# A written-out order for the first batch of an attention and mixer kernel, with filler matmuls, half-column loads and a thinner second batch

## The chip, the cores and the metric

The kernel runs on one core of a Trainium2 chip. A core has five engines that each work through their own instruction list in order and wait for one another by semaphores: TensorE (PE, matmuls; its weight loads are shown apart as PEld), VectorE (DVE), ScalarE (ACT), GpSimd (POOL) and SyncE (SP, which here only issues transfers). Sixteen DMA engines move data between the device memory (HBM) and the on-chip memory (SBUF). Matmuls write to PSUM, an accumulator memory of eight banks, and DVE or ACT must read ("evict") a bank before it can be used again. The metric is the time of one execution on the device in microseconds (us).

## The reference

Two stages follow each other: a cosine attention and a low-rank token mixer with a channel MLP.

```python
# attention: q, k, v are [8 batches, 12 heads, 448 positions, 64]
q_n = q / (np.linalg.norm(q, axis=-1, keepdims=True) + 1e-06)
k_n = k / (np.linalg.norm(k, axis=-1, keepdims=True) + 1e-06)
attn = softmax(np.matmul(q_n, k_n.transpose(0, 1, 3, 2)) / tau)     # tau = 0.1
x = heads_side_by_side(np.matmul(attn, v))                          # [8, 448, 768]
# mixer: U [448, 32], V [32, 448], w_ch1 [768, 3072], w_ch2 [3072, 768]
u = x + ((x.transpose(0, 2, 1) @ U) @ V).transpose(0, 2, 1)
out = u + np.maximum(u @ w_ch1, 0.0) @ w_ch2
```

Inputs and output are float32; matmul operands are bfloat16 on the chip.

## The kernel before

**Units.** The 12 heads of a batch are six *pairs* of heads; there are 48 pairs, numbered through. Pairs are loaded and normalized in *groups*: the first batch has groups of 1, 1, 2 and 2 pairs (g0 to g3), every later batch three groups of 2 (g4, g5, g6 for the second). A group's q, k and v go to staging buffers, of which there are three sets, used in turn (`gi % NST`), so group 3's q can only be loaded once group 0's q has been read.

**Work on a group** (class `Prep`, lines 206 to 269): `square` (ACT or POOL) and `reduce` (DVE) give the squared norms of the rows; `reduce(0)` also clamps them from below (line 240); `root` takes the square root as Exp(0.5 Ln(x)) on ACT; `invert` takes the reciprocal with the temperature folded in (DVE); `scale` multiplies q or k by it and rounds to bfloat16 (DVE or POOL); `values` rounds v (POOL).

**Work on a pair.** `step_T` transposes q and k: by eight PE transposes into a PSUM bank, which DVE copies to SBUF, for the first two batches, and by DMA for the later ones. `step_S` makes scores in four parts, three of two heads by 128 keys and one of the last 64 keys of both heads (c = 3), each evicted by an Exp on ACT. `step_V` multiplies by the values in two halves; its row sums come out beside them, and DVE divides (lines 352 and 353). `step_A`, `step_H` apply the low-rank mixer: A = U^T x is copied to SBUF by ACT, x transposed and A times V are summed in one bank, `up`, and this is evicted to `uE` or `uO` (even and odd batches).

**Mixing pieces.** A batch's channel MLP is 24 pieces of `steps_m1` (six matmuls of 448 columns, and a relu on ACT or DVE, whichever a running estimate finds freer) and 24 of `steps_m2` (six matmuls of 384 columns; four pieces make one output tile of one column half). A piece of the second kind needs rows of w2 of one column half only; a complete output tile needs all 24 row blocks of that half. The pieces of batch b are put into the list `fill` and handed out between the steps of the pairs of batch b + 1 by `spread`, according to the weights in `order`.

**What sets the order.** All five engines run in the order in which the Python code emits instructions. The first batch is emitted by the calls of lines 569 to 683 and has no mixing pieces to put between. The loop of lines 738 to 817 emits the rest, from pair n = 6 on; the dictionary `after` holds the preparation steps of later groups, placed by pair and position with `put`. In the second batch (n = 6 to 11) a pair is given `round(len(fill) / (NP - p + 0.85))` pieces, which is 7 of the 48 for each pair. What is left goes to pair 12.

**Loads.** SP issues the q, k and v loads, except four at the start on ACT, and group 2's k and group 1's v on POOL. POOL issues the weights, which are rounded to bfloat16 on the way: w1 by four blocks of 768 columns (`load_w1`), w2 by four blocks of six row blocks (`load_w2`). POOL's place in the order therefore sets when weights are asked for. Before group 5's loads, `open_loads` writes one element of the staging buffer on DVE so that the loads wait for that.

**PSUM banks.** Scores use four banks (`ps_sc`, two buffers of two banks), the first value half one (`ps_av`), transposes and, after the first batch, `up` one (`ps_x`, one buffer), the mixing pieces two (`ps_m`, two buffers). In the first batch the second value half and `up` also use `ps_m`. The scores of the first two parts of pair 6 are emitted twice: at line 681 and again at line 749.

Of the kernel before, what the change touches and what calls it, by code (L numbers as in the profile page):

```python
# [22 lines left out]
def kernel(  # L23
# [101 lines left out]
    nc.gpsimd.memset(uE[:, :, S:512], 0.0)  # L125

    def load_mixer():
        nc.gpsimd.memset(U_sb, 0.0)
        nc.gpsimd.memset(V_sb, 0.0)
        for t in A_sb:  # L130
            nc.gpsimd.memset(t[64:128, :], 0.0)
        nc.gpsimd.memset(U_raw[64:128, 3, :], 0.0)
        nc.gpsimd.dma_start(out=V_raw[0:R, :], in_=moe_V)
        nc.gpsimd.dma_start(out=U_raw[0:64, :, :], in_=moe_U[0:256].rearrange("(p c) r -> p c r", c=4))
        nc.gpsimd.dma_start(out=U_raw[64:128, 0:3, :], in_=moe_U[256:448].rearrange("(p c) r -> p c r", c=3))
# [25 lines left out]
    def load_w2(n0, n1):  # L161
        nc.gpsimd.dma_start(
            out=w2_sb[:, n0:n1, :],
            in_=moe_w_ch2[n0 * 128:n1 * 128, :].rearrange("(n p) d -> p n d", p=128))
# [41 lines left out]
    class Prep:  # L206


        def __init__(self, gi):
# [4 lines left out]
            self.early = gi < 2  # L214
# [6 lines left out]
        def square(self, j, on_act=False):  # L221
# [6 lines left out]
            if self.early or on_act:  # L228
# [5 lines left out]
        def reduce(self, j):  # L234
# [4 lines left out]
            if j == 0:  # L239
                nc.vector.tensor_scalar_max(out=self.ss[:, :, 0:self.nh * 4],  # L240
                                            in0=self.ss[:, :, 0:self.nh * 4], scalar1=2.0 ** -64)
                est.dve(0.2)

        def root(self):
            s_ = self.ss[:, :, 0:self.nh * 4]
            nc.scalar.activation(s_, s_, AF.Ln)
# [31 lines left out]
    def step_T(b, p):  # L278
        gi, j = group_of[(b, p)]
        qk, _ = norm[gi]  # L280
        t = work.tile([128, 2, 512], BF, name="qkT", tag="qkT", bufs=3)
        qkT[(b, p)] = t
        if by_dma(b * NP + p):
            nc.sync.dma_start_transpose(out=t.rearrange("p a (c r) -> p (a c) r", r=128),
                                        in_=qk[:, j, :, :, :, :].rearrange("p i c h d -> p (i c h d)"))
            return
        tp = psum.tile([128, 8, 128], BF, name="tp", tag="ps_x", bufs=1)
        for i in (1, 0):
            for c in range(4):
                nc.tensor.transpose(out=tp[:, 4 * i + c, :], in_=qk[:, j, i, c, :, :], identity=ident)  # L290
        if b == 0 and p < 2:
            nc.scalar.copy(out=t[:, 1, :].rearrange("p (c r) -> p c r", c=4), in_=tp[:, 4:8, :])
            nc.vector.tensor_copy(out=t[:, 0, :].rearrange("p (c r) -> p c r", c=4), in_=tp[:, 0:4, :])  # L293
        else:
            nc.vector.tensor_copy(out=t.rearrange("p a b -> p (a b)"),
                                  in_=tp.rearrange("p a b -> p (a b)"))
        est.pe(0.46)
        est.dve(0.69)

    def step_S(b, p, cs):  # L300
        t = qkT[(b, p)]
        e = E[(b * NP + p) % 2]
        for c in cs:
            sc = psum.tile([128, 2, 512], FP, name="sc", tag="ps_sc", bufs=2)
            if c == 3:
                nc.tensor.matmul(out=sc[:, 0, 0:S], lhsT=t[:, 1, 384:512], rhs=t[:, 0, 0:S],  # L306
                                 start=True, stop=True)
                nc.scalar.activation(out=e[:, 6, 0:S], in_=sc[:, 0, 0:S], func=AF.Exp)  # L308
                est.pe(0.3)
                est.act(0.56)  # L310
                continue
            for h in range(2):
                r = slice(64 * h, 64 * h + 64)
                nc.tensor.matmul(out=sc[:, h, 0:S], lhsT=t[r, 1, c * 128:(c + 1) * 128],  # L314
                                 rhs=t[r, 0, 0:S], start=True, stop=True)
            nc.scalar.activation(out=e[:, 2 * c:2 * c + 2, 0:S], in_=sc[:, :, 0:S], func=AF.Exp)  # L316
            est.pe(0.25)
            est.act(0.93)
# [3 lines left out]
    def step_V(b, p, half):  # L322
# [5 lines left out]
        X = X_of[(b, p)]  # L328
        if b == 0 and half == 1:
            bank = psum.tile([128, 512], FP, name="mp", tag="ps_m", bufs=2)  # L330
        elif half == 1 and by_dma(b * NP + p):
            bank = psum.tile([128, 512], FP, name="up", tag="ps_x", bufs=1)
        else:
            bank = psum.tile([128, 512], FP, name="av", tag="ps_av", bufs=1)
        av_of[(b, p)] = bank
# [6 lines left out]
        for i in range(2):  # L342
            ic = 2 * half + i
            for h in range(2):
                for c in range(3):
# [4 lines left out]
                                     skip_group_check=True)  # L350
        rd = work.tile([128, 4, 1], FP, name="rd", tag="rd", bufs=4)
# [5 lines left out]
        est.pe(0.52)  # L357
        est.dve(0.6)

# [4 lines left out]
    def step_A(b, p):  # L364
        X = X_of[(b, p)]
        ap = av_of[(b, p)][:, 384:512]
        for c in range(4):
            nc.tensor.matmul(out=ap, lhsT=U_sb[:, c, :], rhs=X[:, c, :],
                             start=False, stop=(c == 3), skip_group_check=True)
        A = A_sb[p % 2]  # L370
        nc.scalar.copy(out=A[0:64, :], in_=ap[0:64, :])
        A_of[(b, p)] = A
        est.pe(0.44)
        est.act(0.3)
        if b == 0:
            up = psum.tile([128, S], FP, name="mp", tag="ps_m", bufs=2)
        else:
            up = psum.tile([128, S], FP, name="up", tag="ps_x", bufs=1)
        up_of[(b, p)] = up
        for c in range(4):  # L380
            n = 128 if c < 3 else 64
            nc.tensor.matmul(out=up[:, c * 128:c * 128 + n], lhsT=X[:, c, :], rhs=ident[:, 0:n],
                             start=(c == 0), stop=False, skip_group_check=True)

    def step_H(b, p):
        up = up_of[(b, p)]
        nc.tensor.matmul(out=up, lhsT=A_of[(b, p)], rhs=V_sb,
                         start=False, stop=True, skip_group_check=True)
        est.pe(0.19)
        if b == 0:  # L390
            nc.scalar.copy(out=u_of(b)[:, p, 0:S], in_=up)
        else:
            nc.vector.tensor_copy(out=u_of(b)[:, p, 0:S], in_=up)
            est.dve(0.62)
# [11 lines left out]
    def step_A2(b, p):  # L406
        ap = av_of[(b, p + 1)][:, 384:512]
# [133 lines left out]
    load(1, "v", nc.gpsimd)  # L541
    load_mixer()
    load(2, "v", nc.sync)


    g0, g1, g2, g3, g4, g5, g6 = preps[0:7]
# [17 lines left out]
    def open_loads(gi):  # L564

        nc.vector.memset(qst[gi % NST][0:1, 0, 0, 0:1], 0.0)
        load_all(gi)

    g0.square(1)
    g0.square(0)  # L570
    g0.reduce(1)
    g0.reduce(0)
    g0.root()
    g1.square(1)
    g1.square(0)
    g0.invert()
    g0.scale(1, 0, V_)
    g0.scale(0, 0, V_)
    g1.reduce(1)
    g2.square(1, True)  # L580
    T(0)
    g2.square(0)
    Sc(0, 0)
    g1.reduce(0)
    g1.root()
    Sc(0, 1)
    g1.invert()
    g1.scale(1, 0, P_)
    g1.scale(0, 0, V_)
    g2.reduce(1)  # L590
    g0.values()
    load_all(3)
    load_w1(0, 768)
    load_w1(768, 1536)
    Sc(0, 2, 3)
    T(1)
    g2.reduce(0)

    Sc(1, 0)
    g2.root()  # L600
    Sc(1, 1)
    g2.invert()
    g2.scale(1, 0, P_)
    g2.scale(0, 0, V_)
    g2.scale(1, 1, P_)
    g1.values()
    load_all(4)
    V(0, 0)
    Sc(1, 2, 3)
    T(2)  # L610
    g3.square(1, True)
# [243 lines left out]
```

## Time and profile before

| | us |
|---|---|
| median of 5 runs (lowest, highest) | 597.29 (596.25, 597.95) |
| the profiled execution | 597.43 |
| its span | 595.6 |
| first transposes on PE | 8.58 |
| first Exp of scores on ACT | 13.40 |
| transposes of pair 4 | 34.90 |
| first mixing piece on PE | 53.24 |
| first matmul of the second kind (w2) | 90.1 |

The span is the stretch that the profiler's records cover; the 1.8 us beside it are start and end. Busy shares are means over stages that differ: in the first batch five engines hand small results to each other, and later PE runs from mixing pieces without a pause. So the profile is read by stretches of time. In a timeline row the columns are start and duration, engine, source line, operation, tiles and shapes, the number of merged instructions, and in brackets how long the engine had been idle and what released it. In a group row the columns are busy time and mean ns of one, then the idle time before these instructions and what ended it.

### The profile page before, as it was taken

The numbers are of one execution on the slowest core, as the hardware profiler recorded it, in microseconds if no ns is written. First come the engines' busy times: TensorE is split into PE (matmuls) and PEld (weight loads), VectorE is DVE, ScalarE is ACT, GpSimd is POOL, SyncE is SP. The second block draws the span as 40 slices with busy tenths as digits, with TensorE's granted clock in tenths as the row PEclk, the third lists the DMA queues.
The fourth block names the chain that finished last, engine by engine and source line by source line (L and its number), as shares of the span: only waits on it lengthen the run. The fifth ranks groups of instructions, "written<-read, shape, count | busy, mean of one in ns | idle before, by whom it ended". The sixth has DMA issues, their size and how long they took to land.

```text
span 595.6 us, 11295 instructions
## 1 busy us (share of the span) xinstructions
PE 567.6 (95%) x4582; PEld 321.6 (54%) x4582; DVE 262.0 (44%) x519; ACT 264.9 (44%) x462; POOL 193.0 (32%) x164
## 2 busy tenths in 40 slices
PE   1678999999999999999999999999999999999997
PEld 0455556655555545555555545555556555555564
DVE  6664576354354264643354263653355342220011
ACT  4784553456443465245442464345532455304300
POOL 7755355354053252252251351350440510000000
PEclk9998999999999999999999999999999999999999
DMA  7999994583564763773545745773645631222022
GB/s 191 205 232 219 232 228 120 124 160 89 117 138 120 159 134 80 155 166 80 133 122 124 160 102 112 147 162 89 135 108 137 141 63 28 45 63 54 1 53 54
DMA packets 135316, 74.18 MB, mean 125 GB/s; under 512 B 85568, under 2 KB 135024, under 8 KB 135264
## 3 DMA queue, kind: packets, MB, share of 16 engines
q1 hardware_dynamic: 128176, 62.83, 46.8%
q0 software_dynamic: 6784, 10.41, 9.5%
q8 instruction: 36, 0.59, 0.4%
q10 hardware_dynamic: 304, 0.21, 0.1%
q14 instruction: 16, 0.13, 0.1%
HBM read 52.19 MB, written 11.01 MB: 106 GB/s over the span
## 4 chain that ended last, share of the span: by engine, by line
PE 91%; DMA 5%; SPq 1%; issue 1%; POOL 1%; ACT 1%; DVE 1%; POOLq 0%
PE mp L480 37%; PE mp L453 37%; PE sc L314 5%; PE av L346 3%; DMA kst<-in_k_dram 2%; PE up L346 2%; PE sc L306 1%; DMA vst<-in_v_dram 1%; PE av L339 1%; DMA qst<-in_q_dram 1%; PE up L339 1%; PE up L412 1%; POOL sq L232 1%; PE av L425 1%; ACT E L316 1%
## 5 line engine op out<-in xcount | busy, mean ns | idle before, releaser
L480 PE MATMUL mp<-w_sb,relu 128*128 128x384 bf16 x1344 | 237.0, 326 | 0.0
L480 PEld LDWEIGHTS <-relu 128*128 128x128 bf16 x1344 | 125.2, 98 | 91.3 <-issue 14.3
L453 PEld LDWEIGHTS <-w_sb 128*128 128x128 bf16 x1152 | 107.4, 98 | 100.6 <-issue 8.9
L316 ACT ACTIVATE E<-sc 128x896 bf16<-128x896 f32 x146 | 126.4, 918 | 68.9 <-PE sc L314 68.7
L457 ACT ACTIVATE relu<-mp 128x448 bf16<-128x448 f32 x164 | 89.3, 544 | 135.5 <-PE mp L453 135.5
L261 POOL TENSOR_TENSOR qk<-kst,inv 128x512 bf16<-128x512 f32 x47 | 58.0, 1254 | 262.0 <-DVE inv L255 252.7
L453 PE MATMUL mp<-uE,w_sb 128*128 128x448 bf16 x576 | 119.3, 353 | 0.0
L453 PE MATMUL mp<-uO,w_sb 128*128 128x448 bf16 x576 | 115.6, 353 | 0.0
L498 DVE TENSOR_TENSOR o_sb<-mp,ut 128x384 f32<-128x384 f32 x50 | 27.8, 557 | 121.7 <-PE mp L480 121.7
L237 DVE TENSOR_REDUCE ss<-sq 128x16 f32<-128x1024 f32 (+1 forms) x50 | 57.3, 1168 | 3.3 <-POOL sq L232 2.1
L261 DVE TENSOR_TENSOR qk<-qst,inv 128x512 bf16<-128x512 f32 x48 | 53.8, 1128 | 0.5
L314 PE MATMUL sc<-qkT 64*128 64x448 bf16 x292 | 42.9, 367 | 7.6 <-DVE qkT L293 4.1
L352 DVE RECIPROCAL rd<-av 128x4 f32<-128x4 f32 x54 | 9.7, 180 | 90.4 <-PE av L346 90.3
L232 POOL TENSOR_TENSOR sq<-qst 128x1024 f32<-128x1024 f32 x23 | 47.1, 2046 | 2.0 <-DMA qst<-in_q_dram 2.0
L232 POOL TENSOR_TENSOR sq<-kst 128x1024 f32<-128x1024 f32 x21 | 41.9, 1998 | 15.6 <-DMA kst<-in_k_dram 10.5
L346 PEld LDWEIGHTS <-E 128*128 128x128 bf16 x1152 | 46.7, 99 | 0.0
L308 ACT ACTIVATE E<-sc 128x448 bf16<-128x448 f32 x48 | 26.0, 542 | 30.8 <-PE sc L306 30.8
L459 DVE TENSOR_SCALAR relu<-mp 128x448 bf16<-128x448 f32 x28 | 17.4, 622 | 35.4 <-PE mp L453 35.1
L269 POOL CAST v<-vst 128x1024 bf16<-128x1024 f32 (+1 forms) x25 | 28.7, 1150 | 9.4 <-DMA vst<-in_v_dram 8.1
L346 PE MATMUL av<-v,E 128*128 128x65 bf16 x648 | 30.1, 196 | 0.0
L339 PEld LDWEIGHTS <-E 128*128 128x128 bf16 x192 | 18.3, 100 | 14.5 <-issue 1.0
L352 DVE RECIPROCAL rd<-up 128x4 f32<-128x4 f32 x36 | 6.5, 181 | 42.7 <-PE up L346 42.6
(97 smaller groups left out, 303.2 us busy)
## 6 DMA issues: line engine op xcount, KB each, us to landing
out_dram<-o_sb SPq DMA_DIRECT2D x112, 96.0 KB, 2.2
w_sb<-in_moe_w_ch_dram POOLq DMA_DIRECT2D x8, 1152.0 KB, 18.5
qst<-in_q_dram SPq DMA_DIRECT2D x23, 256.0 KB, 3.7
vst<-in_v_dram SPq DMA_DIRECT2D x46, 128.0 KB, 2.8
kst<-in_k_dram SPq DMA_DIRECT2D x44, 128.0 KB, 2.7
qst<-in_q_dram SPq DMA_DIRECT2D x23, 192.0 KB, 3.9
vst<-in_v_dram SPq DMA_DIRECT2D x46, 96.0 KB, 2.7
kst<-in_k_dram SPq DMA_DIRECT2D x44, 96.0 KB, 2.6
```

What stands on the lines that cost most here:

```text
L232: nc.gpsimd.tensor_mul(sq[:, 0:self.nh * 4, :], self.flat(t), self.flat(t))
L237: nc.vector.reduce_sum(self.ss[:, j, 0:self.nh * 4], self.sq[j][:, 0:self.nh * 4, :], axis=AX.X)
L261: eng.tensor_mul(qks[self.gi % 2][:, j, i, :, :, :], t[:, 2 * j:2 * j + 2, :, :].rearrange("p h c d -> p c h d"), iv.unsqueeze(3).to_broad ...
L269: nc.gpsimd.tensor_copy(out=self.flat(v65[self.s])[:, :, 0:D], in_=self.flat(vst[self.s]))
L314: nc.tensor.matmul(out=sc[:, h, 0:S], lhsT=t[r, 1, c * 128:(c + 1) * 128], rhs=t[r, 0, 0:S], start=True, stop=True)
L316: nc.scalar.activation(out=e[:, 2 * c:2 * c + 2, 0:S], in_=sc[:, :, 0:S], func=AF.Exp)
L339: nc.tensor.matmul(out=av[:, i, :, :], lhsT=e[:, 6, ic * 128:(ic + 1) * 128], rhs=vv[:, 2 * j:2 * j + 2, 3, :], start=(i == 0), stop=False ...
L346: nc.tensor.matmul(out=av[:, i, h, :], lhsT=e[:, 2 * c + h, ic * 128:(ic + 1) * 128], rhs=vv[:, 2 * j + h, c, :], start=False, stop=(i == ...
L453: nc.tensor.matmul(out=mp, lhsT=w1_sb[:, cc, f * 128:(f + 1) * 128], rhs=u[:, cc, 0:S], start=(cc == 0), stop=(cc == CC - 1))
L457: nc.scalar.activation(out=relu[:, f, o:o + S], in_=mp, func=AF.Relu)
L480: nc.tensor.matmul(out=mp, lhsT=relu[:, f, r0:r0 + 128], rhs=w2_sb[:, f, half * HC:(half + 1) * HC], start=(f == 0), stop=(b > 0 and f == ...
L498: nc.vector.tensor_add(o.rearrange("p (k d) -> p k d", d=128), mp.rearrange("p (k d) -> p k d", d=128), ut_of[(b, half)][:, :, c, :])
```

## The change

Four things change.

1. *The first batch's order.* The steps are split into parts that use one engine each: `pe_T` and `evict_T`, `pe_S` and `exp_S`, `pe_V` and `divide_V`, `pe_A`, `evict_A` and `pe_XT`, `pe_H` and `evict_H`. The calls of lines 569 to 683 are replaced by a list of words, `ORDER`, read by `word`. In it, `sq0k.a` is the square of group 0's k on ACT, `red`, `root`, `inv` and `val` are the other group steps, `sc3q.p` scales q of *pair* 3 on POOL (`.v` on DVE), `l3q` loads q of group 3 on SP, `T4` and `Te4` are the transposes of pair 4 and their eviction, `S31` and `ex31` scores part 1 of pair 3 and its Exp, `V30` and `X30` the first value half and its division, `A3`, `Ac3.v`, `XT3`, `H3`, `U3.a` the mixer parts with the engine of the copy.
2. *Dummy matmuls.* A word such as `w56` emits 56 matmuls of the identity with itself into a PSUM buffer that nothing reads, 166 in all.
3. *w2 by column halves.* `load_w2(half, n0, n1)` loads 384 of the 768 columns of 12 row blocks; both blocks of half 0 are asked for before the last steps of group 4, and half 1 after them.
4. *The second batch* gives five pieces to a pair, with other weights in `order`, and pair 12 takes the other 18. Group 7's loads move from pair 6 to pair 7.

Smaller parts: the clamp of the squared norms is replaced by a bias of the same 2^-64 in the Ln; uE's memset moves behind the first POOL loads; group 1's v is loaded by SP; group 2's v behind group 3's q and k; the squares of g2's and g3's q move from POOL to ACT, which had the other six of g0 to g3; the copies of A and the evictions of `up` are shared between DVE and ACT; `up` of the first batch uses `ps_x` as the transposes do; the memset before group 5's loads goes; and the scores of pair 6 are emitted once.

```diff
+    tiny = const.tile([128, 1], FP, name="tiny")
+    nc.vector.memset(tiny, 2.0 ** -64)
     def load_mixer():
+        nc.gpsimd.memset(uE[:, :, S:512], 0.0)
...
-    def load_w2(n0, n1):
+    def load_w2(half, n0, n1):
+        cols = slice(half * HC, (half + 1) * HC)
         nc.gpsimd.dma_start(
-            out=w2_sb[:, n0:n1, :],
-            in_=moe_w_ch2[n0 * 128:n1 * 128, :].rearrange("(n p) d -> p n d", p=128))
+            out=w2_sb[:, n0:n1, cols],
+            in_=moe_w_ch2[n0 * 128:n1 * 128, cols].rearrange("(n p) d -> p n d", p=128))
...
-            if j == 0:
-                nc.vector.tensor_scalar_max(out=self.ss[:, :, 0:self.nh * 4],
-                                            in0=self.ss[:, :, 0:self.nh * 4], scalar1=2.0 ** -64)
...
-            nc.scalar.activation(s_, s_, AF.Ln)
+            nc.scalar.activation(s_, s_, AF.Ln, bias=tiny)
...
-    load(1, "v", nc.gpsimd)
+    load(1, "v", nc.sync)
     load_mixer()
-    load(2, "v", nc.sync)
...
+    ORDER = """
+        sq0k.a red0k sq0q.a red0q root0 inv0 sq1k.a sc0q.v sc0k.v l3q l3k l2v red1k w56 T0 sq1q.a
+        w11 Te0 sq2k.a red1q S00 S01 ex00 red2k w9 root1 S02 w26 sq2q.a inv1 sc1q.v ex01 red2q
+        val0 l3v ex02 S03 w10 sc1k.v root2 val1 l4q l4k l4v T1 ex03 inv2 place V00 Te1 sc2q.p X00
+        S10 V01 ex10 sc2k.v S11 w1_0 w3 X01 ex11 T2 sc3k.p S12 Te2 A0 sq3q.a S13 Ac0.v XT0 sc3q.p
+        ex12 H0 red3q w9 sq3k.a S20 val2 l5q l5k l5v w8 U0.v ex20 red3k T3 w10 ex13 Te3 root3 S21
+        V10 ex21 inv3 val3 S22 V11 X10 ex22 S23 sc4q.p X11 w5 ex23 S30 A1 ex30 S31 sc4k.v V20
+        Ac1.v ex31 w1_1 T4 sc5q.v S32 V21 Te4 sc5k.p ex32 S33 X20 XT1 ex33 S40 X21 H1 sq4q ex40
+        S41 U1.v A2 V30 Ac2.v ex41 T5 X30 S42 sq4k V31 Te5 ex42 S43 X31 XT2 ex43 S50 red4q A3 ex50
+        S51 w1_2 H2 V40 Ac3.v ex51 S52 U2.v V41 X40 ex52 S53 XT3 X41 H3 ex53 red4k A4 U3.a V50
+        Ac4.a XT4 V51 X50 root4 H4 w1_3 X51 w7 U4.a inv4 A5 Ac5.v XT5 sc6q.v H5 w12 U5.a sc6k.v T6
+        Te6
+    """
+    bank1 = psum.tile([128, 512], FP, name="mp", tag="ps_m", bufs=2)
+    spare = psum.tile([128, 512], FP, name="mp", tag="ps_m", bufs=2)
...
+        elif w[0] == "w":
+            for _ in range(int(w[1:])):
+                nc.tensor.matmul(out=spare[:, 0:128], lhsT=ident, rhs=ident, start=True, stop=True)
+        elif w[0] == "l":
+            load(int(w[1]), w[2], nc.sync)
...
+                pe_V(*at, half, bank1 if half else
+                     psum.tile([128, 512], FP, name="av", tag="ps_av", bufs=1))
...
+    for w in ORDER.split():
+        word(w)
+    load_w2(0, 0, 12)
+    load_w2(0, 12, 24)
+    preps[4].values()
+    preps[4].scale(1, 1, P_)
+    preps[4].scale(0, 1, V_)
+    load_w2(1, 0, 12)
+    load_w2(1, 12, 24)
     fill.extend(steps_m1(0) + steps_m2(0))
...
-            put(NP, 3, lambda gi=gi: load_all(gi))
+            put(NP + gi - 6, 3, lambda gi=gi: load_all(gi))
...
-            nf = len(fill) if last else int(round(len(fill) / (NP - p + 0.85)))
+            nf = len(fill) if last else 5
```

## The prediction

> **What bounds the kernel now.** I read the page first, then the windows of the opening, then the chain in order of time and the timeline, last the groups by form.
>
> ```profile
> PE 567.6 (95%) x4582; PEld 321.6 (54%) x4582; DVE 262.0 (44%) x519; ACT 264.9 (44%) x462; POOL 193.0 (32%) x164
> PE   1678999999999999999999999999999999999997
> DMA  7999994583564763773545745773645631222022
> ```
>
> TensorE (PE) is full from the fifth slice on and idle 28 us in all. The change can only win the start, or lose by opening holes later. The DMA engines are full over the same first six slices.
>
> ```profile
> 8.58:28.56 19.98, 11.57 (x92) 6.93 (x93) 12.81 (x22) 13.95 (x25) 14.18 (x18) 1.00 0.99 211
> 28.56:44.64 16.08, 12.43 (x178) 8.18 (x176) 11.25 (x26) 12.52 (x22) 9.37 (x8) 1.00 1.15 233
> 44.64:53.24 8.60, 5.72 (x63) 4.28 (x62) 5.33 (x14) 4.32 (x11) 6.28 (x7) 0.80 1.15 218
> 53.24:87.00 33.76, 33.53 (x264) 18.24 (x263) 18.71 (x35) 18.94 (x35) 15.20 (x11) 1.00 1.13 234
> ```
>
> Columns: stretch, length, busy time of PE, weight loads, VectorE (DVE), ScalarE (ACT), GpSimd (POOL), granted clock, DMA share, GB/s. Up to 53.24 us no engine is full: DVE has 29.4 of 44.7 us, ACT 30.8. They wait on each other. After 53.24 PE misses 0.2 us in 34.
>
> ```profile
> 34.90 0.61 PE L290 MATMUL tp<-ident,qk 128*128 128x128 bf16 x8
> 50.76 0.55 PE L314 MATMUL sc<-qkT 64*128 64x448 bf16 x4 [0.20 <-DVE qkT L295]
> 52.13 0.37 PE L314 MATMUL sc<-qkT 64*128 64x448 bf16 x2 [0.53 <-ACT E L316]
> 53.24 2.44 PE L453 MATMUL mp<-uE,w_sb 128*128 128x448 bf16 x12
> ```
>
> The first row is the transpose of pair 4. The next two are the same work: scores (6,0) and (6,1) are computed by the opening and again by the loop. The last is the first channel-mixing piece. I measure by the loop's own scores of pair 6: 52.13 us before.
>
> ```profile
> 19.00 6.67 DMA vst<-in_v_dram
> 25.69 14.69 DMA kst<-in_k_dram
> 40.57 3.73 POOL sq L232 x2
> 44.32 1.23 DVE ss L237
> ```
>
> In the chain the opening hangs on loads: group 4's k, behind two w1 quarters, lands at 40.4 us, and squares, reduction, scales and T(6) follow it.
>
> **The change, by the stretches of its order.** Prices:
>
> ```profile
> L316 ACT ACTIVATE E<-sc 128x896 bf16<-128x896 f32 x21 | 18.5, 916 | 4.7 <-PE sc L314 4.7
> L237 DVE TENSOR_REDUCE ss<-sq 128x16 f32<-128x1024 f32 x6 | 7.3, 1212 | 1.3 <-POOL sq L232 1.2
> L261 DVE TENSOR_TENSOR qk<-qst,inv 128x512 bf16<-128x512 f32 x8 | 6.5, 811 | 0.1
> L295 DVE COPY qkT<-tp 128x1024 bf16<-128x1024 bf16 x5 | 3.5, 690 | 3.8 <-PE tp L290 3.8
> L353 DVE TENSOR_TENSOR X<-av,rd 128x256 bf16<-128x256 f32 x6 | 2.5, 425 | 0.2
> ```
>
> *First stretch, to scores (3,1): ACT.* q of group 1 lands at 10.25; its square (0.63) and group 2's k square (1.05) end at 11.95, when the first exp starts (13.40 before). From there ACT holds: pairs 0 to 2, nine exps of 0.92 and three of 0.55 = 9.9; two exps of pair 3, 1.8; three squares, 3.2 (two come over from POOL); three roots of 0.46, 1.4; the four placing copies of U and V, 1.6. Sum 17.9, ending at 29.8; back-to-back exps start every 0.87, so 28.9 to 29.8. The U and T evictions that left ACT now lie on DVE, which has slack here. The removed clamp (0.42, once 1.76) counts only at the head: square root 0.4 us earlier, hidden by the k1 load. Ln's bias tile costs nothing measurable either way; between 0 and one memset (0.06).
>
> *The gate: v of group 3.* `val3` stands ahead of `sc4q.p` on POOL. v3 is issued on SP after l3q, l3k, l2v: 28 issues of about 0.65 put it at 19.6 to 21.6, behind which l4 and l5 queue. Before, v3 was issued at 18.4 to 20.3 and landed up to 28.6, beside a w1 quarter issued at 18.3. The new w1_0 follows `sc2q.p`, at 18.8 by my sum. So v3 lands at 26 (if w1_0 slips a microsecond) to 29; I take 29, the nearest row. Then cast 1.05 and scale 1.3: T4 starts at 31.4 (34.90 before). In the range: 28.2 to 31.5.
>
> *Second stretch, from T4: DVE.* Three qkT copies 2.1; eight X halves with reciprocal, 0.62 each, 5.0; two reductions 2.4; two u evictions 1.2 (0.62, the loop's row); three A copies 0.75 (no DVE row; ACT's 0.25, and 0.42 for the 256-wide division above); inverse 0.55; two scales 1.6. Sum 13.6; ACT has 10.4. T4 itself and hand-overs add 1.5 (0.6 and a dozen of about 0.07). The last scales lie beside POOL's scale of pair 7; such a DVE scale took 0.69 alone and up to 2.34 beside POOL in the second batch: 0 to 3.3, I take 0.8. k4 is no longer late: w1_1 waits behind `sc4q.p` (31.4), so between w1_0's landing (29) and w1_1's first bytes SP has the DMA engines: at 232 GB/s 4 us move 0.9 MB, q and k of group 4. End: 31.4 + 13.6 + 1.5 + 0.8 = 47.3 for scores of pair 6, 4.8 before 52.13.
>
> *Dummies.* 166 matmuls at 0.076 warm (eight transposes, 0.61) or 0.13 cold (1.03): 13 to 22 us in PE's pauses; real work is some 20 of 47 us. Cover gone, the largest, w56, delays nothing: it ends by 8.6, T0 can't start before 8.8. w26 cold costs up to 1. The gain: warm PE steps at half the time (12 value matmuls 0.54 against 0.87). PE is on the path here only in short steps: 0 to 2 us, I take 0 as ACT and DVE bound. At T4 PE stands 3 us without dummies. The row speaks of risk: after 1.72 us of idling at 44.64 the value matmuls took 0.87 again; a cold T4 to S40 would cost 1 us.
> The Trainium skill (TensorE: Matmul & The Clock Gate, Part 1) has the clock fall only after an idle window of about 3.4 us; by it the pause at T4 just passes, and the 1.72 us row disagrees. By the rule the sum stays 47.3, by the row it is 48.3.
>
> *Moves past queues.* v1's four loads go from POOL to SP: POOL is 2.1 us freer (rows of 0.53), SP's l3q is issued at 13.1 as before (13.80), because v2's four go behind l3k. uE's memset (0.42) goes behind POOL's four k2 issues, which start 0.4 sooner; POOL then has nothing due until v0 lands near 14. U and transposes now share one bank: a T waits for the U eviction ahead of it, 0.62, inside DVE's 13.6. The two mixing buffers serve second value halves and dummies; the first mixing piece follows readers that ended 2 us earlier. l5 loses its gating memset and waits for `val2` (POOL, 24) and SP's turn, 28 to 34: earlier than 47.66. The second copy of the pair 6 scores, 0.74 of PE and 1.73 of ACT before 52.13, is already in that mark.
>
> *Second batch.* Five pieces instead of seven per pair move mixing work to pair 12; PE's sum is unchanged, and a pair lasts 3.0 + 5 x 1.2 = 9.0 us instead of 11.4. So g6 and g7 are wanted sooner. Pair n starts about 47.3, 54.7, 63.7, 72.7, 81.7 (n = 6 to 10). POOL's extra issues: w2 halves, twice the rows, 0.84 to 1.7 each (row: 0.84), behind them POOL's value cast and pair 7's k scale, wanted at 52: hidden. w1 and w2 themselves: w1 quarters, from 33.5 at 7.8 each (below), land by 41, 49, 57, wanted at 56 to 79; half 0 of w2 15.6 to 21 later (2.36 MB at 151 to 110 GB/s), 73 to 78, wanted at 88; half 1 by 89 to 98, wanted at 107. With rows the first output would want all 24.
>
> The qkv loads share the engines: between 62.6 and 86.1 three w2 quarters (3.54 MB, 151 GB/s) landed beside group 6 and q of group 7 (1.84 MB, 78 GB/s). At 78 GB/s from 33.5 us: k5 49, k6 67, k7 85. Squares and reductions want k6 at 66, k7 at 80. A reduction waiting in DVE's order holds the X and relu evictions behind it, and through two mp buffers PE. With w2's rows halved the share should pass to SP's loads (k6 65, k7 77): stalls 0 to 6 us, I take 0.9.
> The skill (DMA: Bandwidth & Descriptors, Queues, rings and completion order) says that each engine goes round-robin over its queues by packet; halved w2 packets would then give SP about half, 0 us of stall, and the sum would be 0.9 better. The 34% share above is what the trace has for full rows.
>
> **Sum.** 4.8 - 0.9 = 3.9 us less than the profiled execution's 597.43 (span 595.6 and 1.8 around it; 0.1 above the median): 593.5.
>
> **The rivals.**
> *The order holds without the gate.* v3 lands by 26, T4 at 28.2, DVE's list follows at once: scores at 44 and no stall: gain 8, 589.5. For it: DVE and ACT sums fit; the landing swings by 3 us with 1 us of w1_0. Against: SP has at most eight loads in flight (the 25.69 issue waited for the landing at 25.67) and v3 is twentieth.
> *New waits eat the opening.* Twice as many hand-overs written out one by one, each in-order engine held by the slowest; DVE scales beside POOL at 2 us rather than 0.8: scores at 50 to 51, gain 1 or less, 597. Against: before's own order had 4 us of load wait that is gone.
> *Starved loads, slower.* One mechanism: w1_2 to w2 in one unbroken POOL queue, SP's loads at their 28% share of 18 to 47 us (65 GB/s): k6 at 71, k7 at 91, and DVE stands in red(6) 4 us, in red(7) 6 or more, PE with it: 4.8 - 10 = 5 slower, 602. It decides where k7 lands after 85. For it: before, k6 came only at 75.5 and POOL waited 6.5 us for it. Against: w2's shorter rows.
>
> **How the numbers follow.** The forecast 0.45, no gate 0.25, eaten 0.10, starved 0.20. A change under 0.2% (1.2 us) can't be told here. Faster: 0.43 + 0.25 + 0.04 = 0.72; same 0.08; slower 0.20. The forecast's own range is 591 to 596; the whole reaches 588 (ideal order, 8.9 us) to 600, leaving out half of the starved case and a little below.
>
> **What would show it.** Scores of pair 6 once only, first mixing piece at 47.7; T4 released by `sc4q` on POOL, POOL's cast before it by the v load; 29.8 and no pause on ACT until then; PE rows of 0.54 for value matmuls from pair 0 on. Wrong if mixing starts after 50, or if PE between 60 and 95 us waits for DVE with DVE waiting for POOL's squares and they for k loads.

## The result and the profile after

The changed kernel takes 598.83 us (median; 596.30 to 599.78) against 597.04 us (596.20 to 597.95) for the kernel before, executed beside it: a ratio of 1.0025 (95% interval 1.0019 to 1.0032). It is about 1.8 us slower where 3.9 us faster was forecast. The profiled execution took 599.63 us with a span of 597.8, so it is 0.8 us above its median; that of before took 597.43 with 595.6. The traces below therefore have to explain 2.2 us.

The page of the changed kernel: busy time of PE (share of the span, instructions), then PE and DMA in 40 slices.

```profile
PE 578.4 (97%) x4744; PEld 332.1 (56%) x4744; DVE 255.9 (43%) x499; ACT 266.1 (45%) x456; POOL 185.8 (31%) x157
PE   7788999999999999999999999999999999999996
DMA  6999999453555763672645744763635742223022
```

PE is busier by 10.8 us, mostly with dummies: the first four slices are fuller, and the end is no sooner for it. The windows of the changed kernel, with the same columns as in the prediction:

```profile
8.58:28.56 19.98, 16.90 (x217) 12.42 (x218) 16.95 (x33) 17.81 (x30) 6.24 (x8) 0.91 0.91 191
28.56:44.64 16.08, 12.35 (x140) 8.46 (x140) 7.34 (x19) 7.29 (x10) 13.43 (x12) 0.68 1.07 223
44.64:53.24 8.60, 7.09 (x89) 4.80 (x88) 5.72 (x13) 4.76 (x11) 5.33 (x4) 1.00 1.15 233
53.24:87.00 33.76, 30.58 (x272) 17.30 (x270) 18.77 (x34) 18.77 (x35) 20.09 (x16) 1.00 1.21 239
```

Two rows carry the result. In the second, ACT and DVE do little more than 7 us in 16 (12.5 and 11.3 before) and the granted clock is 0.68: the opening stands still. In the last, PE misses 3.2 us of 33.8, where it missed 0.2 before.

*The opening.* From the chain in order of time of the changed kernel (start, length, what), around the halt:

```profile
18.83 2.10 POOL qk L259 x2
...
22.78 8.63 DMA vst<-in_v_dram
31.56 1.04 POOL v L267
32.60 1.03 POOL qk L259
33.67 0.61 PE tp L288 x4
```

And its timeline: POOL's two value casts, ACT's first Exp after the halt, PE's marks.

```profile
29.23 1.04 POOL L267 CAST v<-vst 128x1024 bf16<-128x1024 f32 x1 [8.31 <-DMA vst<-in_v_dram]
31.56 1.04 POOL L267 CAST v<-vst 128x1024 bf16<-128x1024 f32 x1 [1.29 <-DMA vst<-in_v_dram]
34.81 0.92 ACT L329 ACTIVATE E<-sc 128x896 bf16<-128x896 f32 x1 [6.87 <-PE sc L318]
30.32 0.38 PE L349 MATMUL av<-v,E 128*128 128x130 bf16 x2 [3.52 <-POOL v L267]
33.67 0.61 PE L288 MATMUL tp<-ident,qk 128*128 128x128 bf16 x4 [1.89 <-POOL qk L259]
50.70 0.55 PE L318 MATMUL sc<-qkT 64*128 64x448 bf16 x4 [0.79 <-DVE qkT L293]
```

POOL has no work for 8.31 us, since the cast of group 2's v waits for its load. That load was issued on SP from 18.08 us, just after POOL had asked for the first w1 quarter at 17.91:

```profile
17.91 0.90 POOL L160 DMA_DIRECT2D w_sb<-in_moe_w_ch_dram  x1
18.08 0.60 SPq L202 DMA_DIRECT2D vst<-in_v_dram  x1
```

Group 3's v follows on SP (20.84 to 22.78) and takes 8.63 us. Behind each cast stands a step that PE needs: the value matmuls of pair 2 (a wait of 3.52 us), then the second half of the transposes of pair 4 (T4), for which `sc4q` on POOL comes after `val3`. ACT, which had run ahead, idles 6.87 us. The scores of pair 6 come at 50.70 us instead of 52.13: a gain of 1.4 us, not 4.8.

*The second batch.* All PE pauses of 0.2 us or more between 53.24 and 95 us in the timeline of the changed kernel:

```profile
56.18 0.36 PE L318 MATMUL sc<-qkT 64*128 64x448 bf16 x2 [0.49 <-DVE qkT L293]
66.14 0.36 PE L403 MATMUL up<-ident,X 128*128 128x128 bf16 x4 [1.13 <-DVE qkT L293]
75.48 0.38 PE L389 MATMUL av<-X,U_sb 128*128 128x128 bf16 x4 [0.91 <-DVE X L368]
85.52 0.36 PE L403 MATMUL up<-ident,X 128*128 128x128 bf16 x4 [0.56 <-DVE qkT L293]
94.16 0.38 PE L389 MATMUL av<-X,U_sb 128*128 128x128 bf16 x4 [0.21 <-DVE X L368]
```

Every one waits for DVE's eviction of a transpose or DVE's division. My reading is that with five pieces too little mixing work stands between a PE step and its reader; at 75.48 the division itself stood behind a reduction of 1.21 us on DVE. Over these 41.76 us PE is busy 38.37 us (41.53 before).

The account against the profiled execution of before: 1.4 won up to the scores of pair 6, 3.2 lost to pauses, and some 0.4 us more, of which 0.3 lies behind the last matmul (it ends 4.5 us before the end of the span, 4.2 in the kernel before); 2.2 us in sum. Reckoned from the first mixing piece (51.18 against 53.24) 2.1 are won, and 1.1 are not placed.

### The profile page after: what moved, and what is told of

It reads as the page before. It is cut to its first block, busy times and chain, and to the rows that moved or that the text cites. A ratio compares the mean times of both kernels' runs of the same rounds, so it can differ in the third digit from the quotient of the medians.

```text
span 597.8 us, 11599 instructions
## 1 busy us (share of the span) xinstructions
PE 578.4 (97%) x4744; PEld 332.1 (56%) x4744; DVE 255.9 (43%) x499; ACT 266.1 (45%) x456; POOL 185.8 (31%) x157
## 4 chain that ended last, share of the span: by engine, by line
PE 91%; DVE 3%; DMA 2%; ACT 1%; POOL 1%; SPq 1%; issue 1%; POOLq 0%; DVEq 0%; ACTq 0%
PE mp L510 37%; PE mp L483 36%; PE sc L318 6%; PE av L356 3%; PE up L356 2%; DMA vst<-in_v_dram 1%; PE sc L312 1%; PE av L349 1%; PE up L349 1%; PE up L442 1%; DVE qkT L293 1%; PE tp L288 1%; POOL qk L259 1%; DVE qk L259 1%; ACT E L329 1%
## 5 line engine op out<-in xcount | busy, mean ns | idle before, releaser
L329 ACT ACTIVATE E<-sc 128x896 bf16<-128x896 f32 x144 | 124.8, 917 | 76.1 <-PE sc L318 75.5
L487 ACT ACTIVATE relu<-mp 128x448 bf16<-128x448 f32 x167 | 90.8, 544 | 134.7 <-PE mp L483 134.7
L259 POOL TENSOR_TENSOR qk<-kst,inv 128x512 bf16<-128x512 f32 x43 | 52.8, 1246 | 275.6 <-DVE inv L253 261.6
L259 DVE TENSOR_TENSOR qk<-qst,inv 128x512 bf16<-128x512 f32 x45 | 51.5, 1151 | 0.5
L234 POOL TENSOR_TENSOR sq<-qst 128x1024 f32<-128x1024 f32 x21 | 43.7, 2083 | 0.0
L489 DVE TENSOR_SCALAR relu<-mp 128x448 bf16<-128x448 f32 x25 | 15.6, 623 | 33.8 <-PE mp L483 33.4
L356 PE MATMUL av<-v,E 128*128 128x65 bf16 x648 | 29.8, 195 | 0.0
L349 PEld LDWEIGHTS <-E 128*128 128x128 bf16 x192 | 17.9, 98 | 18.8 <-issue 4.9
```

The costliest lines, as they stand in the source:

```text
L234: nc.gpsimd.tensor_mul(sq[:, 0:self.nh * 4, :], self.flat(t), self.flat(t))
L259: eng.tensor_mul(qks[self.gi % 2][:, j, i, :, :, :], t[:, 2 * j:2 * j + 2, :, :].rearrange("p h c d -> p c h d"), iv.unsqueeze(3).to_broad ...
L349: nc.tensor.matmul(out=av[:, i, :, :], lhsT=e[:, 6, ic * 128:(ic + 1) * 128], rhs=vv[:, 2 * j:2 * j + 2, 3, :], start=(i == 0), stop=False ...
L356: nc.tensor.matmul(out=av[:, i, h, :], lhsT=e[:, 2 * c + h, ic * 128:(ic + 1) * 128], rhs=vv[:, 2 * j + h, c, :], start=False, stop=(i == ...
L487: nc.scalar.activation(out=relu[:, f, o:o + S], in_=mp, func=AF.Relu)
```

## The experiments

The theory after this first reading: (1) the first w1 quarter, asked for ahead of group 2's and group 3's v, delays both and so halts POOL; (2) five pieces per pair are too few to hide DVE's evictions. The rivals: the written order itself is slow (hand-overs, dummies), or the second batch waits for late loads, as the prediction had it.

**The w1 quarter behind the loads.** The word `w1_0` moves behind `sc4q.p`.

```diff
-S11 w1_0 w3 X01 ...
+S11 w3 X01 ...
-... S23 sc4q.p X11
+... S23 sc4q.p w1_0 X11
```

> The changed kernel with one word moved: w1_0, the first quarter of w1, is asked for after sc4q.p instead of after S11, so after v of groups 2 and 3. Theory 1 (v of group 2 and 3 lie in the shadow of w1_0, and val2, val3 hold POOL's in-order queue and with it V20 and sc4q): v2 lands near 23.5 and v3 near 26.5 instead of 29.2 and 31.5, T4 starts near 28.5 instead of 33.7 (its last four transposes), the scores of pair 6 near 46 instead of 50.7; total 4 us below the changed kernel, if the second batch keeps its 3 us of pauses. Rival 1 (the opening is held by DVE's sum and its hand-overs, the load wait only fills time that would be lost anyway): scores of pair 6 within 1 us of 50.7, total unchanged. Rival 2 (w1 asked for later starves the second batch): scores of pair 6 near 46, but PE's pauses between 46 and 95 grow by what was won, total unchanged.

Measured: 596.88 us (594.67 to 602.16), ratio to before 0.9997 (0.9977 to 1.0018). The timeline of this run, POOL's two casts and PE's marks:

```profile
23.20 1.04 POOL L267 CAST v<-vst 128x1024 bf16<-128x1024 f32 x1 [2.04 <-DMA vst<-in_v_dram]
25.77 1.05 POOL L267 CAST v<-vst 128x1024 bf16<-128x1024 f32 x1 [1.53 <-DMA vst<-in_v_dram]
44.12 0.55 PE L318 MATMUL sc<-qkT 64*128 64x448 bf16 x4 [0.79 <-DVE qkT L293]
102.80 0.90 PE L318 MATMUL sc<-qkT 64*128 64x448 bf16 x4 [3.25 <-DMA qkT<-qk]
```

Both casts move up by 6 us and the scores of pair 6 from 50.70 to 44.12: the quarter was the gate. The time falls by only 1.7 us by the ratios. In this profile, which at 599.05 us is 2.2 above the run's median, a thin second batch reaches pair 12 sooner, and its DMA transposes (issue to landing 12.4 us; 4.1 in the changed kernel) run beside the last w2 load: 3.25 us are lost there, besides 3.4 us of pauses between 53.24 and 95 us. How much of this the quicker executions lose isn't shown.

**The second batch as before.** The changed kernel with the weights and the count of the kernel before; the opening is kept.

```diff
-            nf = len(fill) if last else 5
+            nf = len(fill) if last else int(round(len(fill) / (NP - p + 0.85)))
```

The weights in `order` go back with it (2 for most steps).

> The changed kernel with the second batch as before: seven pieces to a pair and the weights of before. Theory 2 (the new weights put no piece behind a transpose, so that the next scores or the next u matmuls wait for its eviction, which DVE does late): PE's pauses between 53 and 95 us fall from 3.2 to under 0.7 us, total 2 to 3 us below the changed kernel, near 596.3. Rival (the pauses come from late k and v loads, as my slower case had it): with the loads at the same place the pauses stay near 3 us or change by under 1 us; total within 1 us of 598.8. A third possibility, that w2 now comes too late for an earlier start of the second kind of piece: pauses move to 85 to 95 us, total unchanged or above.

Measured: 595.34 us (593.01 to 596.25), ratio 0.9957 (0.9941 to 0.9972); PE is busy 41.53 of the 41.76 us from 53.24 to 95, as before; the windows of the changed kernel and of this run:

```profile
53.24:95.00 41.76, 38.37 (x349) 21.75 (x346) 25.33 (x46) 23.80 (x45) 21.54 (x18) 1.00 1.22 238
53.24:95.00 41.76, 41.53 (x352) 23.72 (x351) 24.13 (x43) 20.75 (x37) 19.79 (x16) 1.00 1.22 234
```

The scores of pair 6 come at 49.29 us, still behind the gate (the second half of T4 at 33.64 after a wait of 4.24 us). So 3.5 us of the changed kernel's time, 4.1 by the ratios, go with the thin second batch; 3.2 of them are the pauses. In this profile the opening, which the edit doesn't touch, also ends 1.4 us sooner than in that of the changed kernel.

**Both together:** the late quarter and the second batch as before.

> Both edits. Theories 1 and 2 together: the gains add, 6 to 7 us below the changed kernel, near 592, and 5 us below the kernel before. If the loads of the second batch can't follow a start 5 us earlier with seven pieces to a pair (w1 and w2 wanted sooner, asked for later): PE pauses of 2 to 5 us between 60 and 95 us, total 594 to 596. If rival 1 holds: near 596.

Measured: 589.98 us (589.40 to 590.22), ratio 0.9874 (0.9858 to 0.9889). T4's second half starts at 29.28, the scores of pair 6 at 45.08, and PE is busy 41.53 us of 41.76 again. By the ratios the two edits are worth 1.7 and 4.1 us alone and 9.0 us together: the profile of the first shows its gain being lost at pair 12's transposes, which with seven pieces are issued at 96.85 us instead of 89.93 and land in 5.7 us.

**Without the dummies.** All words such as `w56` are taken out of `ORDER`; nothing else changes.

> The changed kernel without its 166 dummy matmuls. If they buy a warm clock: the value matmuls of pairs 0 to 2 (twelve in 0.54 us) go back to 0.87, each pair of the opening loses under 1 us; since v of group 2 gates V20 at 29.2 to 30.3 anyway, the scores of pair 6 move by less than 1.5 us and the total by 0 to 1.5 us up. If the dummies hold PE's real steps back: total 0.5 us or more below the changed kernel.

Measured: 598.84 us (595.75 to 601.56), ratio 1.0018 (0.9998 to 1.0038). By the median it is the changed kernel's time. In the profiled execution, one of the quicker ones (596.86), the loads landed earlier (group 2's cast at 26.64, scores of pair 6 at 47.95): SP issued group 2's v from 17.11, ahead of the w1 quarter at 17.83 and not behind it. Whether the missing dummies have a part in that isn't shown. The dummies buy nothing that this comparison could tell.

**Five pieces with the old weights,** to separate the number of pieces from where they are put (the changed weights give none behind a transpose).

```diff
-                    (0, not by_dma(n + 1) and (lambda: T(n + 1))),
+                    (2, not by_dma(n + 1) and (lambda: T(n + 1))),
...
             nf = len(fill) if last else 5
```

> The changed kernel with the weights of before in the second batch but still five pieces to a pair. Theory 2a (it is the weight 0 behind a transpose that costs): for even pairs a piece follows T again, for odd pairs five pieces over these weights still leave none between T and A, so of the 3.3 us of listed pauses those of even pairs (0.49 before scores, 0.91 and 0.21 before A) go and those of odd pairs (1.13 and 0.56 before u) stay: 1.5 to 2 us of pauses between 53 and 95, total about 1.5 us below the changed kernel. Theory 2b (five pieces are too few whatever the weights): pauses stay at 3 us or more, total unchanged. If weights alone matter at all places: pauses under 0.7 us, total near that of the seven-piece run, 595.3.

Measured: 600.03 us (598.69 to 600.84), ratio 1.0043 (1.0030 to 1.0056). PE is busy 38.09 us from 53.24 to 95: 3.7 us of pauses in place of 3.4, at the same kinds of steps. Five pieces are enough to cause the pauses, whatever the weights; seven pieces with the changed weights were not run.

**The five-piece second batch in the kernel before.** Count and weights of the change, everything else as before (w2 by rows, old opening).

> The kernel before with the second batch alone changed: five pieces to a pair, the new weights. Theory 2: the pauses come from the spacing and not from the new opening, so 2.5 to 3.5 us of pauses appear between 53 and 100 and the total rises by that, to 600. Rival (they come from loads that run late after the new opening): no pauses, total within 1 us of before.

Measured: 604.73 us (603.25 to 605.50), ratio 1.0118 (1.0101 to 1.0134), where 2.5 to 3.5 us were expected: 7.5 us. The timeline of this run, one row each of POOL, DVE and PE:

```profile
75.91 1.89 POOL L232 TENSOR_TENSOR sq<-kst 128x1024 f32<-128x1024 f32 x1 [7.31 <-DMA kst<-in_k_dram]
77.83 1.22 DVE L237 TENSOR_REDUCE ss<-sq 128x16 f32<-128x1024 f32 x1 [1.62 <-POOL sq L232]
79.66 0.38 PE L368 MATMUL av<-X,U_sb 128*128 128x128 bf16 x4 [2.62 <-DVE X L353]
```

This is the prediction's "starved loads": group 6's k is late, POOL's square waits for it, DVE's reduction for the square, a division stands behind the reduction in DVE's order, and PE waits 2.62 us. Together PE pauses 5.2 us from 53.24 to 95, and the clock granted from 75 to 95 is 0.91, an estimated 1.8 us more. In the changed kernel, which loads w2 by column halves, the square of the same k started at 65.71 after 0.78 us of waiting, and no PE pause goes back to it. The mechanism is real; that the column halves removed it is tested by the next run.

**w2 by rows in the quick version** (late quarter and old second batch).

```diff
-    load_w2(0, 0, 12)
-    load_w2(0, 12, 24)
+    load_w2(0, 6)
+    load_w2(6, 12)
...
-    load_w2(1, 0, 12)
-    load_w2(1, 12, 24)
+    load_w2(12, 18)
+    load_w2(18, 24)
```

> The kernel with w1_0 late and seven pieces to a pair, but w2 loaded by four blocks of rows as before, at the same places of POOL's order. The first output piece wants all 24 row blocks of half 0, near 84 us. If the column halves carry part of the gain: PE waits for w2 near 84 to 90 us, 2 to 6 us, total 592 to 596. If the halves are worth nothing at this pace: w2 by rows lands by 88 at the latest, PE pauses under 1 us, total within 1 us of 590.

Measured: 601.33 us (599.03 to 601.77), ratio 1.0056 (1.0036 to 1.0076): 11.3 us slower than the same kernel with column halves. PE's timeline in this run:

```profile
87.96 1.14 PE L509 MATMUL mp<-w_sb,relu 128*128 128x384 bf16 x6 [2.68 <-DMA w_sb<-in_moe_w_ch_dram]
95.86 2.08 PE L509 MATMUL mp<-w_sb,relu 128*128 128x384 bf16 x6 [6.57 <-DMA w_sb<-in_moe_w_ch_dram]
```

The first output tile needs all 24 row blocks, and PE waits 9.3 us for them; the granted clock from 95 to 105 us is 0.75. The scores of pair 6 come at 43.73 us here, 8.4 sooner than in the kernel before, and the whole is slower than that kernel.

The pair also tells what the halves do to the other loads. POOL's square of group 6's k, with halves and then with rows:

```profile
64.93 1.89 POOL L234 TENSOR_TENSOR sq<-kst 128x1024 f32<-128x1024 f32 x1 [3.60 <-DMA kst<-in_k_dram]
69.08 1.89 POOL L233 TENSOR_TENSOR sq<-kst 128x1024 f32<-128x1024 f32 x1 [7.17 <-DMA kst<-in_k_dram]
```

That of group 7's k starts at 78.22 without a wait, and with rows at 85.96 after 7.05 us. Between 50 and 86 us SP's queue moves 3.85 of 8.52 MB (45%) beside halves and 2.93 of 8.35 MB (35%) beside rows.

**The quick version without dummies.**

> The kernel with w1_0 late and seven pieces to a pair, without dummy matmuls. The load gate that hid them is gone here. If the warm clock matters: PE rows of 0.87 for twelve value matmuls up to pair 1 or 2, scores of pair 6 at 45.5 to 47 instead of 45.1, total up 0.5 to 2 us. If ACT and DVE set the pace: within 0.5 us of 590.

Measured: 588.75 us (588.31 to 591.31), ratio 0.9865 (0.9840 to 0.9890). T4 runs whole at 29.00, the scores of pair 6 at 43.67. Value matmuls are cold (0.87) until about 20 us and warm (0.54) from 25: the cold ones are hidden. The median is 1.2 us below that of the version with dummies, but the intervals of the two ratios overlap.

**The kernel before without its second copy of the pair 6 scores** (line 681).

```diff
-    Sc(6, 0, 1)
     g4.scale(0, 1, V_)
```

> The kernel before, with the second copy of the pair 6 scores left out of the opening (line 681), so that only the loop's copy remains. It asks how much of what the change won up to the scores of pair 6 comes from this one edit. In the kernel before, the first copy stood at 50.76 us and the second at 52.13 us, with 0.74 us of PE and 1.73 us of Exp on ACT between them. Theory 1 (the duplicate lies on the path, since the second copy waits for Exps of the first to free the score banks): the last scores move up by 1.0 to 1.4 us, the first mixing piece starts at about 52.0 (53.24 before), and the total falls by about 1.1 us to 596.2. Theory 2 (the opening is held by the eviction of pair 5's mixing result, which the first piece reads, and the duplicate hides beside it): the first piece stays within 0.3 us of 53.24 and the total within 0.4 us of the kernel before.

Measured: 596.35 us (595.31 to 596.86), ratio 0.9982 (0.9973 to 0.9990); the first mixing piece moves from 53.24 to 52.58. One deleted line is worth 0.6 to 1.6 us. Of the lead of the changed opening, 2.1 us by the first piece (51.18 against 53.24), this edit alone is 0.7 in its profile, though the clock was granted at half for 6.8 us of that opening, and for 3.4 in the kernel before.

**Group 2's v on POOL,** in the changed kernel, with the w1 quarter left in its place.

```diff
     load_mixer()
+    load(2, "v", nc.gpsimd)
...
-... l3q l3k l2v red1k
+... l3q l3k red1k
```

> The changed kernel, except that group 2's v is issued by POOL at the end of load_mixer (POOL idles there from 9.2 to 13.4 us) instead of by SP behind group 3's q and k; the first w1 quarter keeps its place. It tells the place of v2 in SP's queue from the shadow of the w1 quarter. Theory 1 (the quarter issued at 17.9 us slows whatever is issued after it; v2 escapes, v3 does not): group 2's cast on POOL moves from 29.2 to before 24, PE's 3.5 us wait in the value matmuls of pair 2 goes, but v3, now issued at about 18.2 to 20.1, still takes 7 to 9 us, its cast starts at 28 to 29.5, the second half of T4 at 30 to 31.5 (33.67) and the scores of pair 6 at 47 to 48.5 (50.70); the total falls by 2 to 3 us to about 596, since the thin second batch stays. Theory 2 (v2's place alone made the gate): v3 lands by 25, T4 is at 28 to 29.5 as when the quarter is late, scores of pair 6 at 44 to 45.5, and a total near 594, less whatever the second batch gives back. Theory 3 (seven loads at once on the first 12 us delay k and v of groups 0 and 1): first Exp later than 11.9 and no gain.

Measured: 595.94 us (593.55 to 597.36), ratio 0.9976 (0.9964 to 0.9988). POOL in this run:

```profile
20.57 1.04 POOL L267 CAST v<-vst 128x1024 bf16<-128x1024 f32 x1
30.14 1.04 POOL L267 CAST v<-vst 128x1024 bf16<-128x1024 f32 x1 [8.53 <-DMA vst<-in_v_dram]
```

Group 2's cast starts at 20.57 without a wait, but group 3's still at 30.14. T4's second half follows at 32.26 and the scores of pair 6 at 48.70, 0.8 and 0.2 us behind the upper ends of what theory 1 gave, far from theory 2's. With the run of the late quarter this shows the shadow of the w1 quarter as the cause; v2's place only decides how much stands in it.

**A mixing piece ahead of the scores of pair 6.** In every kernel above PE waits 0.79 us for DVE's copy of T6. A call `f(1)` behind the filling of `fill` puts one piece there, in the quick version without dummies and in the one with them.

> The late w1 quarter, the second batch at about seven pieces with the old weights, and no dummies, which gave 588.75; in addition one mixing piece is emitted between the transposes of pair 6 and its first scores, where PE waits 0.79 us for DVE's copy of the transposes. Theory 1 (the pause lies on PE's path and any independent piece fills it): the pause goes, PE's total work is the same, and the time falls by 0.5 to 0.8 us to about 588.1. Theory 2 (the piece itself waits, for the last eviction of pair 5's mixing result or for the first w1 quarter): a pause of similar length stands before the piece, the scores of pair 6 come 1.2 us later than 43.67, and the total stays within 0.3 us of 588.75.

> The same as the run with the piece ahead, but with the 166 dummy matmuls kept: the two differ in the dummies alone. Theory 1 (dummies neither help nor harm, because DVE and ACT set the pace of the opening and PE's cold steps lie beside them): the two totals agree within 0.5 us. Theory 2 (dummies cost: PE must finish a run of them before a step that has become ready, and the clock, granted in full for 0.997 of the run at most, gains nothing): this one is 0.7 to 1.5 us slower, about 589.2. Theory 3 (the warm clock is worth its price once the loads do not gate): this one is 0.7 to 1.5 us faster, about 587.2.

Measured: 588.29 us (587.46 to 591.53), ratio 0.9861 (0.9840 to 0.9883), without dummies; 589.92 us (589.78 to 590.16), ratio 0.9878 (0.9865 to 0.9891), with them. PE's timeline, first without:

```profile
41.82 0.62 PE L288 MATMUL tp<-ident,qk 128*128 128x128 bf16 x8 [0.84 <-DVE qk L259]
42.28 1.30 PE L483 MATMUL mp<-uE,w_sb 128*128 128x448 bf16 x6
43.51 0.55 PE L318 MATMUL sc<-qkT 64*128 64x448 bf16 x4
```

then with dummies:

```profile
42.67 1.03 PE L288 MATMUL tp<-ident,qk 128*128 128x128 bf16 x8 [1.54 <-DVE qk L259]
43.49 2.45 PE L483 MATMUL mp<-uE,w_sb 128*128 128x448 bf16 x6
45.87 0.55 PE L318 MATMUL sc<-qkT 64*128 64x448 bf16 x4
```

Without dummies the 0.79 us pause is gone (the scores have no wait in brackets); the total is 0.5 us lower than without the piece, less than these few executions can tell from nothing. With dummies the median is 1.6 us higher, 1.0 by the ratios, whose intervals overlap. In that profile PE waited 1.54 us behind the last dummies, and T6 and the first piece ran cold. It waited because DVE's two scales took 1.19 and 1.54 us beside POOL's scale, where they took 0.67 and 0.68 without dummies. Group 4's v had landed later, so POOL was later; whether the dummies have a part in that isn't settled. What is shown is that in this execution 166 dummies did not keep the clock up where it counted. The version with the piece and without dummies beats the kernel before by 1.4% and the changed one by 1.6 to 1.8%.

## Why the prediction was wrong

The sign was wrong, though the time lay inside the range of 588 to 600 us. Three terms failed. Between the forecast, 3.9 us below the profiled execution of before, and the measured 2.2 above it lie 6.1 us: 2.3 from the gate, 1.1 from the second stretch, 2.3 from the second batch (3.2 against 0.9), and the 0.4 us more of the account above. By its steps:

*First stretch, ACT: right.* The first Exp came at 11.40 (11.95 forecast, 13.40 before). `ex31` ended at 27.9 (34.81 less the idle 6.87), a microsecond ahead of the 28.9 to 29.8 forecast, and then ACT ran dry. Ln's bias, put at nothing, cost 0.1 us each time (0.31 against 0.21 on 128x16).

*The gate, v of group 3: right place, wrong size.* The failing sentence is "So v3 lands at 26 (if w1_0 slips a microsecond) to 29; I take 29, the nearest row." The release chain (v load, cast, `sc4q`, T4) is the one forecast, but v3 landed at 31.4 and T4 was complete 2.3 us later than the 31.4 forecast. I had costed group 2's v as a place in SP's queue and its cast "(POOL, 24)"; it was cast at 29.23. The quarter went out at 17.91, not 18.8, and SP was a microsecond later than forecast (group 3's q at 14.11, not 13.1), so the quarter stood ahead of all eight value loads instead of beside the last four. I took the nearest row as the upper end, though in the kernel before only group 3's v stood behind the quarter.

*Second stretch, DVE: right in its prices, but it left out the clock.* Forecast 15.9 us from T4 to the scores of pair 6. Measured 17.0 in the changed kernel, at a clock of 0.81, 15.8 in the quick version, at 0.89, and at the full clock 14.7 without dummies, where the window from 29.00 to 43.67 has DVE busy 12.97 us, and 14.5 in the run with w2 by rows. So the sum was 1.2 to 1.4 too high for a warm PE, and that the quick version comes out near it is luck. The prices held; in the groups of the changed kernel over the opening:

```profile
L239 DVE TENSOR_REDUCE ss<-sq 128x16 f32<-128x1024 f32 x6 | 7.3, 1215 | 0.5 <-ACT sq L231 0.5
L259 DVE TENSOR_TENSOR qk<-kst,inv 128x512 bf16<-128x512 f32 x5 | 3.5, 696 | 0.0
L395 DVE CAST A_sb<-mp 64x128 bf16<-64x128 f32 x5 | 1.4, 281 | 0.4 <-PE mp L389 0.4
```

The A copy, which had no DVE row, took 0.28 (0.25 taken). The term for DVE's last scales beside POOL (0 to 3.3, 0.8 taken) was 0 in the changed kernel (0.67 and 0.68 each) and 1.4 in the last run.

*Dummies at 0: right* as far as the medians tell, with and without the gate; but they did not keep the clock. The 1 us named for a cold T4, and left out of the sum, happened and was more: PE stood 3.52 us, the clock in the window that holds T4 was 0.68, T4's second half took 0.61 where four warm transposes take 0.4, and the second stretch took 2.3 to 2.6 us more than with a full clock.

*Second batch: wrong in cause and size.* The term "stalls 0 to 6 us, I take 0.9" meant late k loads. These were forecast well: "k6 65, k7 77", and POOL's squares of them start at 65.71 and 80.41, the latter without a wait. Measured were 3.2 us of pauses, none of it from late loads. The step that failed is the first sentence of the part, "PE's sum is unchanged", taken as if PE's time were then unchanged too: a piece was counted as work only and not as cover. The prediction asked what each removed piece costs later, and never what a DVE eviction of 0.7 us that had lain under two pieces would be laid under with none or one. The window of before had offered the question: 0.2 us of PE pauses beside 24 us of DVE work from 53.24 to 95 us.

*The rivals.* "The order holds without the gate" (scores at 44, 589.5 us) is what the chip does once the quarter is late and the second batch thick: 45.08 and 589.98. "New waits eat the opening" got its number (50 to 51), not its reason. "Starved loads" happened with w2 by rows and a thin second batch, in the opening of before; I had named the column halves as what speaks against it, and the pair of runs that differ in them alone bears that out. The 34% that the prediction reads as SP's share beside full rows is too low: from 62.6 to 86.1 us of the kernel before, SP's queue moved 2.41 of 5.59 MB, 43%.

## What to carry to other kernels

Filler work is also cover: before thinning it, list for each engine's evictions which filler piece hides them, and price what shows when it goes. A large transfer belongs behind the last small load that something waits for, and not just where its queue is free; moving one word here was worth 4 to 7 us of the opening, and 1.7 to 4.9 of the time. Gains of an opening are cashed only if the later suppliers (here w2 by columns, k by group, the transposes of pair 12) are ready sooner too, so change and measure them together.

## What the runs showed of the hardware

- A value load in the opening took 2.8 us from issue to landing (median, quick version) and 8.4 us behind a w1 quarter (changed kernel).
- The clock went to half for whole multiples of 3.4 us. Adding up the granted clock over windows of 0.5 us from 24 us on (from 30 in the kernel before; the view reads 1.00 for the cold start too), PE ran at 0.5 for 3.41 us in the opening of the kernel before, of the quick version and of the last run, for 6.83 in two others (second batch as before; v on POOL) and for 10.24 in the changed kernel.
- The length of the last pause alone did not decide whether it fell. The quick version and the run with w2 by rows both wait 1.81 us ahead of T4's second half, at the same time; in the first the clock fell 1.6 us after that wait, in the second not at all, and its scores of pair 6 come 1.35 us sooner. The first two rows and the first window are of the quick version:

```profile
29.28 0.40 PE L288 MATMUL tp<-ident,qk 128*128 128x128 bf16 x4 [1.81 <-POOL qk L259]
45.08 0.55 PE L318 MATMUL sc<-qkT 64*128 64x448 bf16 x4 [0.79 <-DVE qkT L293]
29.27 0.40 PE L287 MATMUL tp<-ident,qk 128*128 128x128 bf16 x4 [1.81 <-POOL qk L258]
43.73 0.55 PE L317 MATMUL sc<-qkT 64*128 64x448 bf16 x4 [0.79 <-DVE qkT L292]
28.56:44.64 16.08, 14.21 (x195) 10.09 (x195) 11.97 (x30) 9.79 (x16) 14.18 (x13) 0.89 1.05 207
28.56:44.64 16.08, 13.75 (x202) 9.70 (x203) 13.23 (x31) 10.19 (x17) 13.92 (x13) 1.00 1.08 213
```

  It also fell behind a wait of 1.54 us in the last run (granted 0.59 from 42.00 to 44.64). The Trainium skill (TensorE: Matmul & The Clock Gate, Part 1) names an idle window of about 3.4 us, and calls it free-running. The multiples of 3.4 us agree with such a window, and the same pause with two outcomes agrees with its running free; falls behind pauses of 1.54 and 1.81 us do not agree with a window that has to be idle throughout.
- POOL's scale of 1.07 us took 2.25 beside two DVE scales that kept their 0.67 and 0.68; in the last run POOL took 1.49 and DVE 1.19 and 1.54. Alone the three take 2.42 us one after the other; from the first start to the last end they took 2.25 and 2.65 us. So they gain next to nothing by lying side by side; which engine bears the wait differs.
- The changed kernel's executions spread over 3.5 us, those of before over 1.8. No run here tells why, but the profiles have a lead. In four profiles that share the place of the quarter, group 2's v went out on SP 0.17 us behind the quarter (changed kernel), or 0.44, 0.47 and 0.72 ahead of it (second batch as before; five pieces with the old weights; no dummies), and its cast started at 29.23, 27.43, 27.45 and 26.64.
